# Building lists of token numbers on the chip instead of scattering them through DRAM, with w1 and w2 in two transfers each

## The chip, the cores and the metric

The kernel runs on one core of a Trainium2 chip. The engines are TensorE (PE; its weight loads are listed apart as PEld), VectorE (DVE), ScalarE (ACT), GpSimd (POOL) and SyncE (SP). PE's granted clock is 1.2 or 2.4 GHz; the profile gives it as a share of full speed, 0.50 or 1.00 or a mean of the two. The metric is the device time of one execution in microseconds; less is better.

## The reference, cut to what matters

```python
attn_out = _attn_ref(q, k, v)                 # 4 batches, 8 heads, 576 tokens, heads of 64
x = attn_out.transpose(0, 2, 1, 3).reshape(2304, 512)
# _moe_ref: 8 experts, capacity 576
expert_idx = np.argmax(x @ w_gate, axis=1)
for i in range(N):                            # in token order
    e = expert_idx[i]
    if counts[e] < capacity:
        disp[e, counts[e]] = x[i]; pos[i] = counts[e]; counts[e] += 1; keep[i] = True
h = np.maximum(np.einsum('ecd,edf->ecf', disp, w1), 0.0)    # w1 8 x 512 x 1024
y = np.einsum('ecf,efd->ecd', h, w2)                        # w2 8 x 1024 x 512
out[i] = gate_w[i] * y[expert_idx[i], pos[i]]               # kept tokens; others 0
# _moe2_ref
h = x @ w_in                                  # 512 x 2048
r = np.maximum(h, 0.0)
g = s * (r * r) + b
return g @ w_out                              # 2048 x 512
```

In `_attn_ref` keys and values are first averaged over 8 neighbours, so scores are 576 x 72. Of the 2304 tokens of these inputs 1663 are kept: 576, 0, 0, 571, 28, 0, 348 and 140 on the eight experts.

## The kernel before, in words

**Attention** goes through 4 batches of 5 tiles of tokens (128, the last 64). Of each tile it computes scores, values, gate logits, and writes the token's row of 512 values to `xd` in DRAM. For each batch (the last in two parts) `route` gives every token a slot: expert times `capp` plus its place in the expert, ranked by products with a triangular matrix on PE (L338, L340), finished on DVE (`rsf`, then `rsi`). Then POOL makes the token numbers (`iota`, L360) and writes them with an indirect DMA for each tile (L363, `ids<-tok,rsi`) to their slots in the DRAM list `ids`: 128 numbers of 4 bytes for each.

**Units.** The experts' tokens are worked off in units of 288 slots (CH). Units 0 and 1 are picked while attention still runs, after batches 1 and 2 (`pick`, `first.gather`); the other units come from a table that DVE computes once routing is complete (`make`, L595 to L716, ending with `u_ti`). Here there are five units (the last is "wide", 352 columns) and two small ones of up to 144. For each unit SP loads the 288 numbers (`idt`, 3 x 96; `idw` 64 more; `ids_s` for the small ones) from `ids`, and POOL gathers the rows of `xd` by them (`xg<-xd,idt`, L798). PE transposes the rows (`x_part`, L809), ACT and DVE split them into a high and a low part (`xs`, L810, L811), and each layer is three products (high by high, low by high, high by low): `layer1` L818, `layer2` L986. Weights are loaded by SP (`kraw` is w1, `vraw` is w2, each 2 MB in four transfers, L781 and L787) and split by ACT with POOL or DVE. Results go to `yt` in DRAM, and the unit's numbers to `idc` (L992: 288 numbers, from a tile with 96 partitions x 3, so each number is a piece of its own).

**Order.** The order on each engine is the order of the code. `layer1` of unit 0 stands beside the end of attention. `block(u)` is then `layer2` of unit u-1 with `x_part` of u, and `layer1` of u, f running over 8 chunks; beside it stand the splits and the conversion of the last layers' weights (`conv`; its loads `c_raw` are issued by ACT, L827, between ACT's own work). After the units come the small ones (L1099, L1106, L1114) and the last layers: seven blocks of 256 tokens through the second MLP (L912, L1282) with the rows read back from `yt`, scattered to the output by `idc`. `zeros` (L1029) clears the end of `yt` with four transfers.

**Counters.** The transfers that SP and ACT issue use eight counters, here called DMAHW0 to DMAHW7. A transfer that is to use a counter again first waits for the one that used it last, and its engine's queue stands meanwhile.

Of the kernel before, what the change touches and what calls it, by code (L numbers as in the profile page):

```python
# [45 lines left out]
def constants(nc, pool, capp):  # L46
# [24 lines left out]
    c.row0 = pool.tile([P, NB, E], F32, name="row0")  # L71
    nc.gpsimd.iota(c.row0, pattern=[[0, NB], [capp, E]], base=0, channel_multiplier=0, allow_small_or_imprecise_dtypes=True)
# [7 lines left out]
def attention(nc, tc, c, a, cap, capp, left, big, xd, ids, run, hist, first, ps0):  # L80
# [3 lines left out]
    with ExitStack() as es:  # L84
# [163 lines left out]
        def values(i, work=None):  # L248
# [9 lines left out]
            at_pe[0] = o[:, 1, 4 * VW:4 * VW + NB * E].rearrange("p (t e) -> p t e", e=E)  # L258
# [37 lines left out]
        def route(b, t0, t1):  # L296
# [40 lines left out]
            rk = at_pe[0][:, 0:w]  # L337
# [12 lines left out]
            nc.vector.tensor_add(sl, sl, c.row0[:, 0:w])  # L350
# [6 lines left out]
            si = tmp("rsi", [], I32)  # L357
            nc.vector.tensor_copy(si, sf)
            tok = tmp("tok", [], I32)
            nc.gpsimd.iota(tok, pattern=[[P, w]], base=b * S + t0 * P, channel_multiplier=1)  # L360
            for t in range(w):
                n = rows(t0 + t)
                i = nc.gpsimd.indirect_dma_start(out=ids, out_offset=bass.IndirectOffsetOnAxis(ap=si[:n, t:t + 1], axis=0),  # L363
                                                 in_=tok[:n, t:t + 1], in_offset=None, bounds_check=E * capp - 1, oob_is_err=False)
                tc.declare_no_dep(i.ins, group="scatter", reason="slots of different tokens")
                tc.add_to_no_dep_group("scatter", i.ins)
            if t1 == NB and b:

# [22 lines left out]

        o = ps1.tile([P, 2, 512], F32, name="o")
# [25 lines left out]
        for i, (b, t) in enumerate(tiles):  # L418
# [23 lines left out]
            if i == 1:  # L442
                first.fill(one)
# [39 lines left out]
        while todo or scales:  # L483
            more = 7
            while more and todo:
                more -= 1
                if step():
# [4 lines left out]
                    at_pe[0] = o[:, 1, 0:NB * E].rearrange("p (t e) -> p t e", e=E)  # L492
# [11 lines left out]
SSUB = SM // 2  # L504
# [14 lines left out]
class Table:  # L519
# [10 lines left out]
    def __init__(self, nc, pool, cap):  # L530
# [7 lines left out]
        self.st, self.g, self.io, self.iu, self.ie = t("st", [2, 2, E]), t("g", [J, E]), t("io", [J, E]), t("iu", [NV, E]), t("ie", [E, E])  # L538
# [5 lines left out]
        self.left, self.next, self.eq, self.num = t("left", [E]), t("next", [E]), t("eq", [E, E]), t("num", [4])  # L544
# [6 lines left out]
        iota(self.io, [[CH, J], [0, E]], SM)  # L551
        iota(self.iu, [[1, NV], [0, E]])
        iota(self.ie, [[0, E], [1, E]])
        iota(self.e1, [[1, E]], 1)

    def pick(self, nc, i, tot, rev, cap, capp):
# [28 lines left out]
        v.tensor_copy(self.i[i], f)  # L585

    def make(self, nc, hist, capp):
# [73 lines left out]
        units = lambda out, x: (v.tensor_tensor(out=out[:, :NV], in0=self.iu, in1=row(x[:, 0], NV), op=ALU.is_ge),  # L661
                                v.tensor_tensor(out=out[:, NV:], in0=self.ie.rearrange("p a b -> p b a"), in1=row(x[:, 1], E), op=ALU.is_ge))
# [5 lines left out]
        v.tensor_sub(mine, mine, cmp)  # L668
        ex, slot, col, new = (self.tab[:, i] for i in range(4))
# [23 lines left out]
        v.tensor_sub(ch, self.iu[:, :, 0], self.s2[:, 0:NV])  # L693
# [22 lines left out]
        v.tensor_copy(self.ti, self.tab)  # L716

# [31 lines left out]
class Experts:  # L749
# [4 lines left out]
    def __init__(self, nc, tc, c, a, left, m, xd, ids, idc, yt, hist, cap, capp):  # L754

        self.__dict__.update({k: v for k, v in locals().items() if k != "self"})
        self.t = Table(nc, left, cap)
# [11 lines left out]
        self.idt = [m.tile([SUB, NSUB], I32, name=f"idt{i}") for i in range(3)]  # L769
        self.w1v = a["moe_w1"].rearrange("e (k p) (f c) -> e p f k c", p=P, c=2 * P)  # L770
        self.w2v = a["moe_w2"].rearrange("e (f p) d -> e p f d", p=P)
        self.ids_s = [m.tile([SSUB, 2], I32, name=f"ids_s{i}") for i in range(4)]
# [6 lines left out]
    def load_w1(self, src):  # L779
        for i in range(KF // 2):  # L780
# [145 lines left out]
    def main(self, left, one, ps):  # L926
# [561 lines left out]
```

## Time and profile before

| | |
|---|---|
| three runs | 705.03, 713.31, 713.93 us, median 713.31 |
| the profiled execution | 706.86 us, span 705.1 us, mean granted clock 0.93 |
| busy: PE, DVE, ACT, POOL | 594.7, 382.1, 254.3, 324.2 us |
| attention | 0 to 122 us |
| unit 0, layer 1, beside the end of attention | 122 to 145 us |
| block 1, 2, 3, 4 | from 145, 185, 222, 268 to 302 us |
| small units and the last unit's layer 2 | 302 to 381 us |
| last layers: their start, then the rest | 381 to 424, 424 to 697 us |

A stage's PE busy time beside its length tells how much PE idles there; the row before a piece of idle time names what ended it. The profiled execution took 6.45 us less than the median of the three runs.

### The profile page before, as it was taken

Reading aid. Unit: us, or ns where it says so; the run is one execution under the profiler, and the core shown is the slowest. Engines: PE = TensorE matmul, PEld = TensorE weight load, DVE = VectorE, ACT = ScalarE, POOL = GpSimd, SP = SyncE. Lnnn points to the kernel's source line nnn. Section 1 sums busy time; section 2 is a strip of 40 time slices with the busy share of each in tenths; the row PEclk is TensorE's granted clock in tenths of the full one; section 3 lists DMA queues with packets and bytes.
Section 4 is the critical chain, followed back from the end, with each engine's and each line's share of the span. In section 5 each row is a group of like instructions: output and inputs, shape, how many; then the busy total and the mean of one; then the engine's idle time right before and its main releaser. Section 6 shows DMA issues by size and latency. Waiting matters only on the chain. (4 is left out here: it accounts for less than half of the span.)

```text
span 705.1 us, 11212 instructions
## 1 busy us (share of the span) xinstructions
PE 594.7 (84%) x3943; PEld 551.3 (78%) x3943; DVE 382.1 (54%) x793; ACT 254.3 (36%) x617; POOL 324.2 (46%) x336
## 2 busy tenths in 40 slices
PE   6887869769599387995879669989999999999985
PEld 5786768658499387995878648887989989899875
DVE  4686877949589382444422976998322113021150
ACT  1363645435254244424312634331413304123030
POOL 5566744565363343502310975544563515335291
PEclk8798998979889798999889879999999999999999
DMA  8998998692538776494824910001720100100000
GB/s 170 196 174 152 137 156 238 155 281 61 97 92 185 240 169 211 55 278 124 272 51 125 381 51 1 0 1 45 269 91 16 31 30 1 46 17 2 33 2 18
DMA packets 78572, 81.98 MB, mean 116 GB/s; under 512 B 30732, under 2 KB 59404, under 8 KB 78476
## 3 DMA queue, kind: packets, MB, share of 16 engines
q1 hardware_dynamic: 67580, 67.19, 37.7%
q0 software_dynamic: 3184, 6.83, 4.5%
q10 hardware_dynamic: 7712, 6.84, 3.3%
q8 instruction: 41, 0.67, 0.5%
q14 instruction: 55, 0.45, 0.4%
HBM read 64.04 MB, written 17.62 MB: 116 GB/s over the span
## 5 line engine op out<-in xcount | busy, mean ns | idle before, releaser
L1282 PE MATMUL bank<-wo,gh 128*128 128x512 f32 (+1 forms) x448 | 135.5, 385 | 15.3 <-POOL wo L1256 9.2
L1277 POOL TENSOR_TENSOR gl<-rt,gh 128x256 fp32r<-128x256 f32 (+1 forms) x112 | 89.4, 807 | 88.0 <-ACT gh L1276 80.7
L1282 PEld LDWEIGHTS bank<-wo,gh 128*128 128x128 f32 x448 | 83.6, 193 | 34.2 <-POOL wo L1256 11.1
L1282 PE MATMUL bank<-wo,gl 128*128 128x512 f32 (+1 forms) x224 | 85.7, 382 | 0.0
L791 POOL TENSOR_TENSOR w1l<-kraw,w1h 128x512 fp32r<-128x512 f32 x40 | 54.1, 1367 | 60.9 <-ACT w1h L790 60.6
L986 PE MATMUL bank<-hs,w2h 128*128 128x288 f32 (+1 forms) x308 | 73.4, 328 | 6.8 <-issue 6.8
L986 PEld LDWEIGHTS bank<-hs,w2h 128*128 128x128 f32 x308 | 55.4, 209 | 7.6 <-issue 7.3
L1289 DVE SCALAR_TENSOR_TENSOR raw<-bank,sb,c_u 128x512 f32<-128x512 f32 (+1 forms) x14 | 9.9, 710 | 85.4 <-PE bank L1282 85.4
L1270 ACT ACTIVATE rt<-tq 128x256 f32<-128x256 f32 (+1 forms) x26 | 9.6, 368 | 114.5 <-PE tq L912 92.7
L1282 PEld LDWEIGHTS bank<-wo,gl 128*128 128x128 f32 x224 | 43.3, 193 | 7.7
L986 PE MATMUL bank<-hs,w2l 128*128 128x288 f32 (+1 forms) x148 | 47.1, 318 | 0.0
L1276 ACT CAST gh<-rt 128x256 fp32r<-128x256 f32 (+1 forms) x112 | 43.0, 384 | 4.2 <-DVE rt L1271 4.1
L1271 DVE SCALAR_TENSOR_TENSOR rt<-bank,rt 128x256 f32<-128x256 f32 (+1 forms) x60 | 24.1, 402 | 36.1 <-ACT rt L1270 36.1
L1290 POOL DMA_INDIRECT out_dram<-raw,it x12 | 12.0, 1000 | 62.6 <-DVE raw L1289 62.1
L1270 ACT ACTIVATE rt<-bank 128x256 f32<-128x256 f32 (+1 forms) x60 | 22.2, 370 | 39.2 <-PE bank L912 26.2
L1256 POOL TENSOR_TENSOR wo<-c_f,wo 128x512 fp32r<-128x512 f32 x16 | 24.8, 1550 | 21.5 <-ACT wo L1255 21.5
L210 PE MATMUL sc<-kbd,qT 128*128 128x144 f32 (+1 forms) x152 | 26.3, 324 | 8.9 <-DVE r L267 6.2
L795 DVE TENSOR_TENSOR w2l<-vraw,w2h 128x512 fp32r<-128x512 f32 x39 | 32.3, 829 | 1.5 <-POOL tok L360 1.3
L798 POOL DMA_INDIRECT xg<-xd,idt x15 | 17.8, 1189 | 32.4 <-DMA idt<-ids 29.6
L986 PEld LDWEIGHTS bank<-hs,w2l 128*128 128x128 f32 x148 | 30.9, 209 | 0.0
L210 PEld LDWEIGHTS sc<-kbd,qT 128*128 128x128 f32 (+1 forms) x152 | 22.6, 206 | 10.5 <-issue 9.6
L255 PE MATMUL o<-vx,eT 128*128 128x146 f32 (+1 forms) x144 | 24.4, 317 | 6.6 <-DVE u_sum L569 3.1
(409 smaller groups left out, 1672.0 us busy)
## 6 DMA issues: line engine op xcount, KB each, us to landing
kraw<-in_moe_w_dram SPq DMA_DIRECT2D x24, 512.0 KB
vraw<-in_moe_w_dram SPq DMA_DIRECT2D x24, 512.0 KB
wo<-in_moe_w_out_dram SPq DMA_DIRECT2D x16, 512.0 KB
c_raw<-in_moe_w_in_dram ACTq DMA_DIRECT2D x13, 512.0 KB
kraw<-in_k_dram SPq DMA_DIRECT2D x8, 576.0 KB
out_dram<-c_u SPq DMA_DIRECT2D x1, 4608.0 KB
q<-in_q_dram SPq DMA_DIRECT2D x16, 256.0 KB
xd<-xr SPq DMA_DIRECT2D x16, 256.0 KB
```

Source lines behind the costliest of these rows:

```text
L210: nc.tensor.matmul(sc[:n, p // 2, p % 2 * 144:p % 2 * 144 + 144], lhsT=q[:, p, :n], rhs=kbd[b % 2][:, p], start=True, stop=True)
L255: nc.tensor.matmul(o[:n, p // 2, p % 2 * 2 * VW:p % 2 * 2 * VW + 2 * VW], lhsT=et[:, p, :n], rhs=two_cols(vx[g][:, 2 * p:2 * p + 2]), star ...
L791: eng.tensor_sub(self.w1l[:, i], self.w1(i), self.w1h[:, i])
L795: eng.tensor_sub(self.w2l[i], self.w2r[:, i], self.w2h[i])
L798: self.nc.gpsimd.indirect_dma_start(out=self.xg[u % 2][:, s], out_offset=None, in_=self.xd[:rows], in_offset=bass.IndirectOffsetOnAxis(ap= ...
L986: nc.tensor.matmul(py[d][:, :v.n], lhsT=l[f][:, d * P:d * P + P], rhs=r[f], start=f == 0 and i == 0, stop=f == KF - 1 and i == 2)
L1256: nc.gpsimd.tensor_sub(w[:, 1], f, w[:, 0])
L1270: nc.scalar.activation(r, p, AF.Relu)
L1271: nc.vector.scalar_tensor_tensor(out=r, in0=p, scalar=0.0, in1=r, op0=ALU.max, op1=ALU.mult)
L1276: nc.scalar.copy(gh[:, at, :n], rt[f % 4][:, :n])
L1277: nc.gpsimd.tensor_sub(gl[:, at, :n], rt[f % 4][:, :n], gh[:, at, :n])
L1282: nc.tensor.matmul(p[:, c], lhsT=l[:, at, j * P:j * P + P], rhs=wo[f][:, z, c], start=f == 0 and i == 0, stop=f == KF2 - 1 and i == 2)
```

## The change

Four things change. **The lists.** `ids` in DRAM goes, with its scatters and the loads `idt`, `idw`, `ids_s`. For each batch POOL now divides the slot into a multiple of 96 and a remainder (six small operations on `rsf`) and makes two one-hot matrices for each tile, `ohq` (128 x 48: which row of 96) and `ohp` (128 x 96: which place in it, times the token's number). PE adds `ohq` transposed times `ohp` over the tiles (L394), and DVE adds that to `u_lists`, 48 rows of 96 numbers in SBUF. A unit's numbers are a selection of rows by a further product: `picked` (L631) for units 0 and 1, `numbers` (L642) for all others at once, after the table; DVE turns them into indices in SBUF that the gathers use directly. **The store to `idc`** comes from a tile with rows of 96 numbers (L879): three pieces of 384 bytes for a unit, not 288 of 4 bytes. **w1 and w2** come in two transfers of 1 MB each, not four of 512 KB; rows of w1 are 2 KB, not 1 KB. **`zeros`** is one transfer, not four, and `idc` is filled at the start. `capp` falls from 864 to 576. The units of these inputs stay the same.

```diff
@@ route
-            si = tmp("rsi", [], I32)
-            nc.vector.tensor_copy(si, sf)
-            tok = tmp("tok", [], I32)
-            nc.gpsimd.iota(tok, pattern=[[P, w]], base=b * S + t0 * P, channel_multiplier=1)
+            g = nc.gpsimd
...
+            g.tensor_scalar(out=qi, in0=sf, scalar1=1.0 / SUB, scalar2=None, op0=ALU.mult)
+            g.tensor_scalar(out=key, in0=qi, scalar1=float(-SUB), scalar2=None, op0=ALU.mult)
+            g.tensor_add(lo, key, sf)
+            g.tensor_scalar(out=key, in0=lo, scalar1=0.0, scalar2=float(SUB), op0=ALU.is_lt, op1=ALU.mult)
+            g.tensor_add(lo, lo, key)
+            g.tensor_sub(key, sf, lo)
+            g.iota(tok, pattern=[[P, w]], base=b * S + t0 * P, channel_multiplier=1, allow_small_or_imprecise_dtypes=True)
             for t in range(w):
-                n = rows(t0 + t)
-                i = nc.gpsimd.indirect_dma_start(out=ids, out_offset=bass.IndirectOffsetOnAxis(ap=si[:n, t:t + 1], axis=0),
-                                                 in_=tok[:n, t:t + 1], in_offset=None, bounds_check=E * capp - 1, oob_is_err=False)
...
+                g.tensor_scalar(out=ohq[:, t], in0=q96, scalar1=key[:, t:t + 1], scalar2=None, op0=ALU.is_equal)
+                g.tensor_scalar(out=ohp[:, t], in0=p96, scalar1=lo[:, t:t + 1], scalar2=tok[:, t:t + 1], op0=ALU.is_equal, op1=ALU.mult)
...
+            n = at_pe[0][:nq, NB * E:NB * E + SUB]
+            for t in range(w):
+                m = rows(t0 + t)
+                nc.tensor.matmul(n, lhsT=ohq[:m, t], rhs=ohp[:m, t], start=t == 0, stop=t == w - 1)
+            lists = first.t.lists
+            if b:
+                nc.vector.tensor_add(lists, lists, n)
+            else:
+                nc.vector.tensor_copy(lists, n)
+            if last and b < B - 1:
...
+                first.t.picked(nc, b - 1, at_pe[0][:SUB, NB * E + SUB:NB * E + SUB + 4])
+                while scales:
+                    scale()
+                first.gather(b - 1, b * S + S)
@@ Table
+    def picked(self, nc, i, p):
+        nc.tensor.matmul(p, lhsT=self.lists, rhs=self.sel[:self.lists.shape[0]], start=True, stop=True)
+        nc.vector.tensor_add(self.pf[:SUB, i], p, self.over[:SUB])
+        nc.vector.tensor_copy(self.idx01[:SUB, i], self.pf[:SUB, i])
...
+    def numbers(self, nc, c, p, rows):
...
+        nc.tensor.matmul(p[:SUB, 0:w], lhsT=self.lists, rhs=sel[:n], start=True, stop=True)
+        nc.vector.scalar_tensor_tensor(out=idx[:SUB], in0=over[:SUB], scalar=float(BIG), in1=p[:SUB, 0:w], op0=ALU.mult, op1=ALU.add)
+        yield
+        nc.vector.tensor_copy(self.idx[:SUB].rearrange("p u s -> p (u s)"), idx[:SUB])
+        yield
+        nc.tensor.transpose(p[:w, P:P + SUB], idx[:SUB], c.ident[:SUB, :SUB])
+        nc.scalar.copy(rows[:w], p[:w, P:P + SUB])
@@ make, at its end
         v.tensor_copy(self.ti, self.tab)
+        four = lambda x: x.unsqueeze(2).to_broadcast([P, NV + E, 4])
+        sel, over, s4 = (self.flat(z).rearrange("p (u s) -> p u s", s=4) for z in (mine, cmp, p2))
+        v.tensor_tensor(out=s4, in0=four(slot), in1=self.at.unsqueeze(1).to_broadcast([P, NV + E, 4]), op=ALU.add)
+        yield
+        v.tensor_tensor(out=over, in0=s4, in1=four(self.lim), op=ALU.subtract)
+        v.tensor_scalar(out=sel, in0=s4, scalar1=self.p96, scalar2=None, op0=ALU.is_equal)
+        yield
+        v.tensor_scalar(out=over, in0=over, scalar1=self.atp[:, 0:1], scalar2=0.0, op0=ALU.add, op1=ALU.is_ge)
@@ Experts
     def load_w1(self, src):
-        for i in range(KF // 2):
+        for i in range(KF // 4):
             self.nc.sync.dma_start(out=self.w1r[:, i], in_=src[:, i])
     def load_w2(self, src, i):
-        self.nc.sync.dma_start(out=self.w2r[:, i:i + 2], in_=src[:, i:i + 2])
+        self.nc.sync.dma_start(out=self.w2r[:, i:i + 4], in_=src[:, i:i + 4])
...
-    def load_ids(self, u, slots):
-        self.nc.sync.dma_start(out=self.idt[u % 3], in_=slots.rearrange("(s p) o -> p (s o)", p=SUB))
+    def gather(self, u, have):
+        for s in range(NSUB):
+            self.rows(self.xg[u % 2][:, s], self.t.idx01[:, u, s:s + 1], have)
+    def store_numbers(self, u, i, n, rows):
+        self.nc.sync.dma_start(out=self.idc[bass.ds(self.regs[u][1], n * SUB)].rearrange("(s p) o -> s (p o)", p=SUB), in_=rows[4 * i:4 * i + n])
...
-            nc.sync.dma_start(out=self.idc[cols(u, ids.shape[1] * sub)].rearrange("(s p) o -> p (s o)", p=sub), in_=ids)
...
-            for k in range(KD):
-                nc.sync.dma_start(out=yt[k * P:k * P + P, bass.ds(self.kept, 2 * CU)].rearrange("p (n c) -> p n c", c=CU),
-                                  in_=zf.unsqueeze(1).to_broadcast([P, 2, CU]))
+            nc.sync.dma_start(out=yt.rearrange("(d p) n -> p d n", p=P)[:, :, bass.ds(self.kept, 2 * CU)], in_=zf.unsqueeze(1).to_broadcast([P, KD, DM]))
@@ block
+                    lists = self.t.numbers(nc, self.c, px[0], rows)
+                if u == 1 and f > 4:
+                    next(lists, None)
+                if u == 1 and f == 7:
+                    tokens(2, 0)
...
-                if u == 1 and 0 <= f - 3 <= NSUB:
-                    tokens(2, f - 3)
+                if u == 1 and f < NSUB:
+                    tokens(2, f + 1)
```

On POOL, batch 0 before: the two operations of its list stand between the pooling of keys and of values.

```order
L138 TENSOR_TENSOR kraw<-kraw 72x4x128
L140 TENSOR_TENSOR kp<-kraw 72x256
L360 IOTA tok_842 128x5
L363 DMA ids<-tok_842,rsi_840 7008x1 x5
L136 TENSOR_TENSOR vraw<-vraw 128x4x256
L138 TENSOR_TENSOR vraw<-vraw 128x4x128
```

The same place now; the pair L374, L375 stands five times.

```order
L147 TENSOR_TENSOR kp<-kraw 72x256
L366 TENSOR_SCALAR rqi_851<-rsf_838 128x5
L367 TENSOR_SCALAR rkey_853<-rqi_851 128x5
L368 TENSOR_TENSOR rlo_852<-rkey_853,rsf_838 128x5
L369 TENSOR_SCALAR rkey_853<-rlo_852 128x5
L370 TENSOR_TENSOR rlo_852<-rlo_852,rkey_853 128x5
L371 TENSOR_TENSOR rkey_853<-rsf_838,rlo_852 128x5
L372 IOTA tok_854 128x5
L374 TENSOR_SCALAR ohq<-q_198,rkey_853 128x48
L375 TENSOR_SCALAR ohp<-p_199,rlo_852,tok_854 128x96
L374 TENSOR_SCALAR ohq<-q_198,rkey_853 128x48
L375 TENSOR_SCALAR ohp<-p_199,rlo_852,tok_854 128x96
```

Seventeen instructions stand where there were six, and PE has a product (L394) behind them. On PE the end of layer 1 of unit 0 now holds the last ranks and list of batch 3 in this order, ahead of block 1's first product (L1047).

```order
L894 MATMUL misc<-xs,w1l 128x288
L345 LDWEIGHTS tri
L345 MATMUL o<-roh_1844,tri 128x16
L347 LDWEIGHTS ones
L347 MATMUL o<-roh_1844,ones 128x8
L348 LDWEIGHTS ones
L348 MATMUL o<-run,ones 128x16
L383 LDWEIGHTS ones
L383 MATMUL o<-run,ones 128x8
L394 MATMUL o<-ohp,ohq 48x96 x2
L1282 MATMUL tq<-ident,u_pf 8x96
L1047 MATMUL bank_1901<-hs,w2h_162 128x288 x2
```

Before, the ranks of the first part of batch 3 (L338) stood after the first of the eight chunks of that layer, and those of the second part after the fourth; now the first stand after the fifth and the second at the very end, and a list (L394) follows each. On ACT, block 3 before (waits in brackets; DMAHW are the transfers' counters): between two pieces of `xs` stands a load of `c_raw` that waits for a counter.

```order
L810 CAST xs<-tq 128x288 [waits DVE_49,PE_49]
L790 CAST w1h<-kraw 128x512 [waits DMAHW3_49,Pool_49]
L737 ACTIVATE c_u_1894<-c_raw_1114 128x512 [waits DMAHW0_49]
L827 DMA c_raw_1029<-in_moe_w_in_dram 128x4x256 [waits DMAHW2_49,Activation_49]
L810 CAST xs<-misc 128x288 [waits DVE_49,PE_49]
L790 CAST w1h<-kraw 128x512 [waits Pool_49]
```

On SP just ahead of block 3 now: one transfer of zeros (L1084), then w2 (L859) in two; the loads of `idt` and `idw` that stood ahead of the zeros are gone.

```order
L1084 DMA yt<-raw_1917 128x4x512 [waits DMAHW6_49,DMAHW2_49,DVE_49]
L1257 COMPARE_AND_BRANCH
L1036 TENSOR_LOAD u_ti
L1036 ISA x2
L1095 COMPARE_AND_BRANCH
L859 ISA
L859 DMA vraw<-in_moe_w_dram 128x4x512 [waits DMAHW0_49,DMAHW7_49,DVE_49,Activation_49]
```

ACT's load there still waits for DMAHW2, but w2 uses counters 0 and 1, and DMAHW2 belongs to the store of unit 1's results, half a block earlier.

## Rows read from the trace of the kernel before

**Rows 1.** Windows: length; PE, PEld, DVE, ACT, POOL busy; PE clock, DMA share, GB/s
```profile
76.00:122.00 46.00, 39.46 (x298) 36.05 (x296) 36.17 (x121) 26.52 (x55) 23.72 (x22) 0.93 1.05 178
...
222.00:268.00 46.00, 28.88 (x206) 28.20 (x204) 28.06 (x36) 16.11 (x35) 16.25 (x12) 0.85 0.80 228
268.00:302.00 34.00, 33.43 (x216) 32.60 (x217) 13.72 (x24) 17.10 (x37) 14.67 (x12) 0.95 0.52 110
...
424.00:697.00 273.00, 264.56 (x1722) 240.14 (x1720) 108.96 (x184) 78.23 (x229) 124.83 (x146) 1.00 0.11 38
```

**Rows 2.** Timeline of PE: start, length, work, idle time before it and its releaser
```profile
74.86 1.24 PE L255 MATMUL o<-vx,eT 128*128 128x146 f32 x8 [2.41 <-DVE rsf L355]
...
98.92 1.24 PE L255 MATMUL o<-vx,eT 128*128 128x146 f32 x8 [3.08 <-DVE u_sum L569]
...
151.90 0.42 PE L809 MATMUL tq<-ident,xg 96*128 96x96 f32 x1 [3.21 <-DMA xg<-xd,idt]
...
176.62 0.53 PE L818 MATMUL bank<-xs,w1h 128*128 128x288 f32 x2 [2.07 <-DVE hs L821]
...
190.29 0.39 PE L809 MATMUL tq<-ident,xg 96*128 96x96 f32 x1 [4.90 <-DMA xg<-xd,idt]
...
240.25 0.74 PE L809 MATMUL misc<-ident,xg 96*128 96x96 f32 x3 [11.05 <-DVE xs L811]
...
267.95 0.82 PE L986 MATMUL bank<-hs,w2h 128*128 128x288 f32 x2 [5.93 <-issue]
...
335.05 1.22 PE L1114 MATMUL bank<-rt,vraw 128*128 128x144 f32 x8 [3.48 <-issue]
...
361.16 5.14 PE L1114 MATMUL bank<-rt,vraw 128*128 128x144 f32 x20 [3.67 <-issue]
```

**Rows 3.** Waits of PE: releaser, us in total, times, longest
```profile
PE tq L809 <- DMA xg<-xd,idt: 12.8, 5, 4.9
...
PE bank L1106 <- DVE yr L1100: 3.9, 2, 2.8
```

**Rows 4.** Timeline of DVE: the first and the last of the table's work in block 1
```profile
165.17 1.38 DVE L647 TENSOR_TENSOR u_tri<-u_key 128x128 f32<-128x128 f32 x1
...
176.00 0.20 DVE L716 CAST u_ti<-u_tab 128x76 int32<-128x76 f32 x1
```

**Rows 5.** Timeline of ACT in block 3
```profile
239.31 0.40 ACT L810 CAST xs<-misc 128x288 fp32r<-128x288 f32 x1 [13.93 <-DMA vraw<-in_moe_w_dram]
```

**Rows 6.** Timeline of SP's transfers from block 2 to block 3: start, length of the issues
```profile
210.34 0.43 SPq L992 DMA_DIRECT2D idc<-idt  x1
...
223.57 0.34 SPq L803 DMA_DIRECT2D idt<-ids  x1
...
229.02 3.67 SPq L1029 DMA_DIRECT2D yt<-rt  x4
234.03 2.32 SPq L787 DMA_DIRECT2D vraw<-in_moe_w_dram  x4
```

**Rows 7.** Windows before, in and after the time that follows a store of `idc`
```profile
205.00:212.00 7.00, 7.00 (x55) 7.00 (x54) 6.83 (x7) 4.04 (x9) 6.47 (x6) 1.00 0.60 183
213.00:221.00 8.00, 8.00 (x63) 8.00 (x62) 8.00 (x12) 4.70 (x10) 3.19 (x3) 1.00 0.70 53
222.00:228.00 6.00, 6.00 (x51) 6.00 (x50) 5.41 (x9) 2.45 (x6) 1.28 (x1) 1.00 1.08 352
...
288.00:303.00 15.00, 15.00 (x95) 15.00 (x94) 9.91 (x17) 8.33 (x17) 3.43 (x3) 1.00 0.58 44
```

**Rows 8.** Groups of instructions by line on POOL: busy us, mean ns, idle before
```profile
L363 POOL DMA_INDIRECT ids<-tok,rsi x20 | 20.1, 1003 | 13.4 <-issue 6.3 <-DVE xr L293 6.0 <-POOL tok L360 0.8
...
L70 POOL TENSOR_SCALAR pen<-pen 128x40 f32<-128x40 f32 x1 | 0.3, 324 | 0.0
```

**Rows 9.** The chain that ended last, its first two pieces: start, us
```profile
373.21 7.28 DMA idc<-ids_s
380.63 4.35 DMA wo<-in_moe_w_out_dram
```

More of the change, by code (lines that the diff above doesn't have):

```diff
@@ L77, in rows, with attention @@
     return P if t < NB - 1 else S - (NB - 1) * P
-def attention(nc, tc, c, a, cap, capp, left, big, xd, ids, run, hist, first, ps0):
+def attention(nc, tc, c, a, cap, capp, left, big, xd, run, hist, first, ps0):
     with ExitStack() as es:
@@ L390, in attention @@
         pool_all("k", 0, 7, 8, nc.gpsimd)
+        first.nc.sync.dma_start(out=first.idc.rearrange("(p n) o -> p (n o)", p=SUB), in_=big_ids)
         o = ps1.tile([P, 2, 512], F32, name="o")
@@ L679, in make @@
         v.memset(new, 0.0)
+        v.tensor_tensor(out=p2[:, 0:NV + E], in0=mine, in1=row(self.ends, NV + E), op=ALU.mult)
         v.tensor_reduce(out=ex, in_=ohe, axis=AX.X, op=ALU.add)
@@ L683, in make @@
         yield
+        v.tensor_reduce(out=self.lim, in_=p2[:, 0:NV + E], axis=AX.X, op=ALU.add)
         v.tensor_tensor(out=new[:, 1:], in0=ex[:, 1:], in1=ex[:, :NV + E - 1], op=ALU.not_equal)
@@ L827, in load_raw @@
             queue.dma_start(out=self.c_raw[i % 3].rearrange("p (k c) two -> p k (c two)", k=KD), in_=self.w_in64[:, (KF + i) % KF2])
-    def fill(self, pool):
-        nc = self.nc
-        for d, w in ((self.ids, E * self.capp // SUB + 1), (self.idc, (T + 2 * CH) // SUB)):
-            z = pool.tile([SUB, w], I32, name=f"z{w}")
-            nc.gpsimd.iota(z, pattern=[[1, w]], base=BIG, channel_multiplier=0)
-            nc.sync.dma_start(out=d.rearrange("(p n) o -> p (n o)", p=SUB), in_=z)
     def beside(self, i, pool):
@@ L891, in unit1 @@
         self.picked(1)
-        for s in range(NSUB):
-            self.gather(1, s, T - S)
     def load_y(self, u):
@@ L940, in main @@
         wide = self.Parts(WIDE, mem[:2 * KD], mem[2 * KD:])
-        idw = [left.tile([MORE, 1], I32, name=f"idw{i}") for i in range(3)]
         self.it = [left.tile([P, 2], I32, name=f"it{i}") for i in range(4)]
@@ L947, in main @@
         yo = lambda i, n: ys[:, i * KD * CH:i * KD * CH + KD * n].rearrange("p (k c) -> p k c", k=KD)
-        zf = self.rt[0]
+        zf = self.raw[0]
+        rows, rows01 = (self.yr[:, i, SM:SM + SUB].bitcast(I32) for i in range(2))
         xs = self.yr[:, :, 0:SM]
@@ L1041, in block @@
                 with if_new(u - 2):
-                    for f in range(0, KF, 2):
+                    for f in range(0, KF, 4):
                         self.load_w2(w2s(u), f)
@@ L1128, in to_small @@
             small_gather(0)
-            if v is wide:
-                nc.sync.dma_start(out=self.idc[CH:][cols(u, MORE)], in_=idw[u % 3])
             with if_new(self.t.NV):
@@ L1168, in last @@
             early = cap >= SM + CU
+            small_numbers(s)
             if early:
@@ L1449, in program @@
         xd = dr.tile([T, DM], F32, name="xd")
-        ids = dr.tile([E * capp + SUB, 1], I32, name="ids")
         idc = dr.tile([T + 2 * CH, 1], I32, name="idc")
@@ L1458, in program @@
             with tc.tile_pool(name="m", bufs=1, side="right") as m:
[L1459 to L1460 removed]
+                x = Experts(nc, tc, c, a, left, m, xd, idc, yt, hist, cap, capp)
+                ps = attention(nc, tc, c, a, cap, capp, left, m, xd, run, hist, x, ps0)
                 w = es.enter_context(tc.tile_pool(name="w", bufs=1))
```

169 lines of the change are left out of this document (95 added, 74 removed).

## The prediction

> **What bounds the kernel now.** I read the windows by stage first. From 424 us on, PE is busy 264.56 of 273 us at full clock [rows 1]: nothing in this change touches that, so whatever comes must come from the 424 us ahead of it. In block 3 (222 to 268 us) PE is busy only 28.88 of 46 us, at a granted clock of 0.85, and block 4 next to it is full (33.43 of 34) [rows 1]. So the second view was PE's timeline there. Two holes make up 17 us: 11.05 us ahead of an `x_part` product, and 5.93 us at the block's end [rows 2]. The first is put down to DVE's `xs`, which waits for ACT's `xs`, which sat 13.93 us until a load of w2 (`vraw`) had landed [rows 5]. ACT's `xs` needs no w2. What needs it is the load of `c_raw` that stands ahead of it on ACT: it waits for the counter DMAHW2, last used by w2, as the order of ACT shows. And w2 was late because SP issued it only at 234.03 us, behind four transfers of zeros that went out from 229.02 to 232.69, behind `idt` at 223.57 and `idw` [rows 6]. The second hole ends on "issue", with another such `c_raw` load ahead of the work that PE waits for.
>
> The third view was the rate of the transfers. After SP stores `idc` at 210.34 us [rows 6], the rate falls from 183 to 53 GB/s for 8 us though the DMA engines are 0.70 busy, then rises to 352; after the wide unit's store it is 44 GB/s for 15 us at a share of 0.58 [rows 7]. Busy engines that move little are moving small pieces: the 288 numbers are 288 pieces of 4 bytes. The scatters of `ids` are 128 such pieces each. I call this the crawl. The last store of that kind heads the chain that ended last: 7.28 us, and only then does the load of `wo` (4.35 us) start that the last layers wait for [rows 9].
>
> **The change part by part**, against the profiled execution, 706.86 us.
>
> *Block 3's holes.* The changed order has one transfer of zeros, no `idt` or `idw` ahead of w2, and ACT's load of `c_raw` waits for the counter of a store that went out half a block earlier. I take both holes as gone, 11.05 + 5.93, and of the low clock beside them 1.5 us: −18.5. Next in line there is the split of w1 on ACT and POOL; block 4, which does the same work, has no such hole [rows 1]. A load of w1 or w2, now 1 MB in a piece, lands later at its first half: 512 KB more at 183 to 352 GB/s [rows 7] are 1.5 to 2.9 us. If that falls at the head of both halves of a block, and the clock with it, half the gain is left: −9 is the smaller bound.
>
> *Waits for gathers.* PE waited 12.8 us in five pieces for gathers of units 1 and 2 [rows 3], whose lists were scattered, read back, then used. Now indices stand in SBUF and this goes, −12.8 before what replaces it.
>
> *What replaces it.* POOL's price for a small operation is 0.32 us (a tensor_scalar of 128 x 40), that of a scatter 1.0 us [rows 8]. A list of five tiles is 17 operations of 0.3 us and 0.07 us between dependent ones, 6.3 us; before it was 5 scatters and their gaps, 6.4 us. POOL's time is neutral, but before nobody waited for it, and now PE stands in order at L394.
> - Batch 0: `rsf` comes at 74.86 us [rows 2], the list at about 81, and PE arrives one tile later, at 76.6: +4.5.
> - Products L394 (20 tiles), L631, L642, and DVE's adds: 0.25 us a tile by the three 96 x 96 transposes of 0.74 us [rows 2], half of it beside other waits: +2.
> - End of layer 1 of unit 0: ranks, total and list of batch 3 now stand at the end of the row, and PE waits for DVE's slots and POOL's one-hots of the second part, some 4 us for the first list (three tiles, 4.8 us of POOL) and 6 for the second. +10.
> - Table: its bulk on DVE runs from 165.17 to 176.20 [rows 4], and PE waited 2.07 us for DVE behind it [rows 2]. Now eight more operations of 0.2 to 0.3 us stand there, and PE stands at L642 after the sixth chunk until they are done, 10.5 us where it could go on before; the 2.07 go. +8.5.
>
> Sum from 145 to the start of block 3: 10 + 8.5 − 12.8 = +6 (rounded), with bounds of −5 (DVE finds its inputs earlier and PE waits little) and +15 (each list takes twice as long).
>
> *The crawl gone.* The stores are now three pieces of 384 bytes, the scatters none. In attention the 3.08 us at 98.92 [rows 2] stood behind a store of `xr` in the crawl of batch 1's scatters: −3. After the stores of the small units, PE waits 3.48 and 3.67 us for "issue" [rows 2], time in which instructions come late; I take −5 of these and a third, smaller one. PE waited 3.9 us for `yr` at the small unit's start [rows 3], again behind ACT and a w2 load: −4. At the last layers' start `wo` no longer waits out the 7.28 us [rows 9]; a contiguous store still takes 2 to 3: −4.5. Half-clock time after the holes that go, beyond what block 3 has: −4. Together −20.5.
>
> One rule speaks against this. The Trainium skill, "DMA: Bandwidth & Descriptors", section Specifications, gives 512 B as the least transfer for line rate and says that below this the engine does a read-modify-write. The new pieces, 384 bytes, are still below it; by that rule alone the crawl would stay, and the sum would be 20.5 us worse but for the yr wait. The rows show only 4-byte pieces, and there are 96 times fewer now, so I take their number as what costs and leave the other reading to a rival.
>
> *w1 and w2 in half as many transfers.* Same bytes; a 2 KB row moves little faster than two of 1 KB, and SP's queue is not what fills the time. The gain is the counters, counted above. Nothing else.
>
> Sum: −18.5 + 4.5 + 2 + 6 − 20.5 = −26.5, so 680 us on the profiled execution's basis. The median of the three runs stands 6.45 us above it and two of the three lie there, so I add 6: **686 us**.
>
> **The rivals.** 2% of 713.31 (about what a measurement here can tell from no change) puts the borders at 699.0 and 727.6.
>
> *The crawl stays.* Small pieces, those of 384 bytes included, hold the queues as before whatever their number, and only the counters' waits go. For it: the rows cannot tell number from size. Against it: 3 pieces instead of 288. (It is what the rule of the Trainium skill above would make of these stores.) Then the −20.5 shrinks to −4 (the `yr` wait is one of counters): −10, 697 on the profile's basis, 703 on the median's: within 2%.
>
> *The units end earlier but the last layers do not start earlier.* Conversion of their weights on DVE, ACT and POOL stands between the units' work and may fill the time instead; in block 3 DVE is busy 28.06 of 46 us [rows 1], so without the holes it is nearly as full as PE. If half of block 3's gain and half of the crawl's is lost that way: 686 + 9 + 10 = 705; if only block 3's, 695. I take 697.
>
> *Slower: PE waits for POOL's one-hots.* Four lists stand on PE's path (batch 0, batch 2 beside layer 1, two of batch 3). If a small POOL operation costs 1.0 us, as an indirect transfer does [rows 8], a list of five takes 17 us, not 6.3, and one of three 13. That is +10.7 for batch 0 and for batch 2 (whose cover is one chunk of 2 us, gone then), +8 and +6 for the others, 35 us, and as much as 5 more of table start: −26.5 + 40 = +13.5, 727 on the median's basis, the border of slower. It decides from about 0.75 us an operation, where the sum is zero. For it: POOL spans stretch beside a busy DVE. Against it: 0.32 us measured.
>
> **How the numbers follow.** Forecast .66, of which nearly all lies under 699 (its own range 668 to 699); last layers not earlier .14 (697, half under 699, half over); the crawl stays .13 (703, a third under 699); slower .07 (727, and .05 of it beyond 727.6). Faster: .63 + .08 + .04 = .75; same .20; slower .05. The lower end is every listed hole gone with new waits at their lower bounds: 686 − 11 − 9 − 4 = 662; the upper one takes in the crawl's rival, 706.
>
> **What would show it.** Right: no PE hole over 3 us from 222 to 302 us of the old order; no window of 8 us under 60 GB/s at a DMA share over 0.5 behind a store of `idc`; a PE wait of 4 to 5 us for POOL at L394 in batch 0, of 8 to 12 us for DVE at L642; no wait for gathers of units 1 and 2. Wrong would make me: `c_raw` loads on ACT that still wait for w2; POOL operations beyond 0.6 us; the crawl behind three pieces of 384 bytes; or a larger gain in attention, where DMA share is 1.05 from 76 to 122 us [rows 1], if the transfers, not PE's chain, set its length.

## The result, and the profile after

The changed kernel took 679.5 us (median of 4 runs, 678.86 to 680.74), the kernel before in the same runs 711.82: a ratio of 0.9564, 95% interval 0.9495 to 0.9632. The profiled spans are 677.1 and 705.1 us, 28.0 less. The forecast was 686, from −26.5 on the profiled execution. Where the sets of runs below hold slow runs of the kernel before (over 1.5% above its fastest), the medians count them and the ratios leave them out.

First the page of the changed kernel: PE's line, PE's clock in 40 slices, and the packets.

```profile
PE 598.0 (88%) x3991; PEld 550.0 (81%) x3991; DVE 386.9 (57%) x814; ACT 254.6 (38%) x619; POOL 330.0 (49%) x391
...
PEclk8798699886789998999999779999999999999999
...
DMA packets 65887, 81.92 MB, mean 121 GB/s; under 512 B 24698, under 2 KB 40058, under 8 KB 65793
```

PE's work has not shrunk, 598.0 us against 594.7; its share rose because the span fell. Where the time went is read from the starts of the stages in the two timelines of PE:

| stage starts at (first product of) | before, us | after, us | stage that ends here: after less before, us |
|---|---|---|---|
| layer 1 of unit 0 (L818, now L894) | 129.16 | 129.19 | 0.0 |
| block 1 (L986, now L1047) | 144.47 | 159.34 | +14.8 |
| block 3 | 221.84 | 230.79 | −5.9 |
| block 4 | 267.95 | 260.97 | −15.9 |
| small units (L1106, now L1163) | 317.49 | 310.70 | +0.2 |
| last layers (L912, now L974) | 371.92 | 348.73 | −16.4 |
| their second layer (L1282, now L1344) | 402.61 | 373.85 | −5.6 |
| end of span | 705.1 | 677.1 | +0.8 |

So the stage in which the lists are finished became twice as long, and the change pays in block 3, the small units and the start of the last layers. The rows of PE's timeline in the changed kernel that answer to [rows 2] (idle time and its releaser in brackets):

```profile
76.09 0.55 PE L394 MATMUL o<-ohp,ohq 128*48 128x96 f32 x2 [1.06 <-POOL ohp L375]
...
145.71 0.37 PE L394 MATMUL o<-ohp,ohq 128*48 128x96 f32 x2 [2.57 <-POOL ohp L375]
...
157.30 0.55 PE L394 MATMUL o<-ohp,ohq 128*48 128x96 f32 x2 [3.66 <-POOL ohp L375]
...
185.18 0.60 PE L642 MATMUL tq<-u_mine,u_lists 48*96 48x76 f32 x2 [13.26 <-DVE u_mine L788]
...
260.97 0.51 PE L1047 MATMUL bank<-hs,w2h 128*128 128x288 f32 x2 [2.98 <-issue]
...
320.62 1.22 PE L1171 MATMUL bank<-rt,vraw 128*128 128x144 f32 x8 [1.92 <-issue]
...
340.91 4.16 PE L1171 MATMUL bank<-rt,vraw 128*128 128x144 f32 x32 [1.60 <-issue]
```

No hole of 11 us is left in block 3, and the 5.93 at its end are 2.98; the waits for "issue" among the small units have halved ("issue" means that the profile shows nothing that the engine waited for). In their place stand waits for POOL's one-hots and one of 13.26 us for the table. What the waits for the lists do to the clock is in the windows of the same kernel, columns as in [rows 1]:

```profile
140.00:145.00 5.00, 3.14 (x24) 2.91 (x22) 3.35 (x13) 2.15 (x5) 3.97 (x11) 1.00 0.68 221
145.00:150.00 5.00, 3.11 (x13) 2.35 (x14) 1.01 (x6) 0.83 (x2) 2.75 (x5) 0.60 0.00 2
150.00:155.00 5.00, 1.96 (x11) 1.58 (x9) 2.29 (x14) 1.13 (x2) 0.65 (x3) 0.50 0.14 52
155.00:160.00 5.00, 2.02 (x8) 1.25 (x9) 0.25 (x1) 0.69 (x3) 3.56 (x10) 0.50 0.78 254
```

From 143 us PE works and waits by turns, and the granted clock falls from 1.00 to 0.50: the chunk of layer 1 in the middle of it runs at half speed as well.

SP's transfers and the windows behind the store of `idc` answer to [rows 6, 7]:

```profile
219.19 0.34 SPq L879 DMA_DIRECT2D idc<-yr  x1
221.24 4.13 SPq L853 DMA_DIRECT2D kraw<-in_moe_w_dram  x2
227.00 0.41 SPq L1084 DMA_DIRECT2D yt<-raw  x1
228.53 6.05 SPq L859 DMA_DIRECT2D vraw<-in_moe_w_dram  x2
```

```profile
218.00:226.00 8.00, 7.93 (x61) 7.70 (x59) 7.86 (x8) 4.42 (x12) 6.55 (x6) 1.00 0.82 268
226.00:234.00 8.00, 8.00 (x62) 8.00 (x63) 8.00 (x17) 5.32 (x12) 0.17 (x1) 1.00 1.04 315
234.00:245.00 11.00, 10.92 (x86) 10.69 (x85) 10.90 (x15) 7.06 (x16) 9.42 (x7) 1.00 1.02 349
```

Where 53 GB/s followed the store before, 268 and 315 follow it now. The first transfer of w2 goes out 1.5 us after the zeros.

The chain that ended last no longer has a store of `idc` at the last layers' start:

```profile
349.33 3.21 DMA yt<-yo
...
352.80 4.06 DMA wo<-in_moe_w_out_dram
```

It waits 3.21 us for the last results' store, where it waited 7.28 [rows 9].

### The profile page after: what moved, and what is told of

Read it like the earlier page. It is cut to its first block, busy times and chain, and to the rows that moved or that the text cites. A ratio compares the mean times of both kernels' runs of the same rounds, so it can differ in the third digit from the quotient of the medians.

```text
span 677.1 us, 11128 instructions
## 1 busy us (share of the span) xinstructions
PE 598.0 (88%) x3991; PEld 550.0 (81%) x3991; DVE 386.9 (57%) x814; ACT 254.6 (38%) x619; POOL 330.0 (49%) x391
## 4 chain that ended last, share of the span: by engine, by line
PE 42%; DVE 20%; issue 6%; POOL 3%; DMA 3%; ACT 2%; SPq 0%; DVEq 0%; another core or an unknown queue 0%; ACTq 0%; POOLq 0%
PE bank L1344 13%; PE bank L974 7%; PE bank L1047 6%; DVE c_f L1367 4%; PE tq L974 4%; PE misc L974 4%; PE bank L894 3%; DVE c_f L814 2%; DVE w2l L867 2%; DVE c_f L812 1%; DVE c_f L809 1%; PE misc L894 1%; PE tq L894 1%; DVE c_f L818 1%; POOL gl L1339 1%
## 5 line engine op out<-in xcount | busy, mean ns | idle before, releaser
L1344 PE MATMUL bank<-wo,gh 128*128 128x512 f32 (+1 forms) x448 | 136.3, 387 | 11.7 <-POOL wo L1318 8.5
L1344 PEld LDWEIGHTS bank<-wo,gh 128*128 128x128 f32 x448 | 83.9, 194 | 30.8 <-POOL wo L1318 10.5
L1344 PE MATMUL bank<-wo,gl 128*128 128x512 f32 (+1 forms) x224 | 86.2, 385 | 0.0
L863 POOL TENSOR_TENSOR w1l<-kraw,w1h 128x512 fp32r<-128x512 f32 x40 | 52.6, 1331 | 47.3 <-ACT w1h L862 46.9
L1047 PE MATMUL bank<-hs,w2h 128*128 128x288 f32 (+1 forms) x308 | 71.3, 321 | 3.2 <-issue 3.0
L1047 PEld LDWEIGHTS bank<-hs,w2h 128*128 128x128 f32 x308 | 53.3, 202 | 4.2 <-issue 3.6
L1344 PEld LDWEIGHTS bank<-wo,gl 128*128 128x128 f32 x224 | 43.6, 195 | 7.9
L1047 PE MATMUL bank<-hs,w2l 128*128 128x288 f32 (+1 forms) x148 | 46.2, 312 | 0.0
L871 POOL DMA_INDIRECT xg<-xd,u_idx x24 | 26.3, 1094 | 24.3 <-DVE u_idx L645 10.9
L867 DVE TENSOR_TENSOR w2l<-vraw,w2h 128x512 fp32r<-128x512 f32 x39 | 30.4, 779 | 1.4 <-ACT w2h L866 1.0
L1047 PEld LDWEIGHTS bank<-hs,w2l 128*128 128x128 f32 x148 | 29.8, 201 | 0.0
L1367 DVE TENSOR_TENSOR c_f<-c_f,wo 128x512 f32<-128x512 f32 x30 | 26.3, 877 | 0.8
```

What stands on the lines that cost most here:

```text
L863: eng.tensor_sub(self.w1l[:, i], self.w1(i), self.w1h[:, i])
L867: eng.tensor_sub(self.w2l[i], self.w2r[:, i], self.w2h[i])
L871: self.nc.gpsimd.indirect_dma_start(out=dst, out_offset=None, in_=self.xd[:have], in_offset=bass.IndirectOffsetOnAxis(ap=idx[:n], axis=0), ...
L1047: nc.tensor.matmul(py[d][:, :v.n], lhsT=l[f][:, d * P:d * P + P], rhs=r[f], start=f == 0 and i == 0, stop=f == KF - 1 and i == 2)
L1344: nc.tensor.matmul(p[:, c], lhsT=l[:, at, j * P:j * P + P], rhs=wo[f][:, z, c], start=f == 0 and i == 0, stop=f == KF2 - 1 and i == 2)
L1367: nc.vector.tensor_add(sums["acc"], sums["acc"], wo[i // 2][:, i % 2])
```

## The experiments

All times are medians; "before" is the kernel before on the same chip in the same runs; a set is what ran on one chip together. The kernel before moved from set to set (711.8, 714.3, 724.0, 719.7, 724.5), so kernels are compared within a set, or by their ratio.

**The small pieces put back.** In the changed kernel the numbers go to `idc` from the tile of 96 partitions x 3 again.

```diff
-        self.nc.sync.dma_start(out=self.idc[bass.ds(self.regs[u][1], n * SUB)].rearrange("(s p) o -> s (p o)", p=SUB), in_=rows[4 * i:4 * i + n])
+        idx = self.t.idx01[:, u] if isinstance(u, int) and u < 2 else self.t.idx[:, i]
+        self.nc.sync.dma_start(out=self.idc[bass.ds(self.regs[u][1], n * SUB)].rearrange("(s p) o -> p (s o)", p=SUB), in_=idx[:SUB, 0:n])
```

> The changed kernel, with one thing undone: the numbers go to idc from the tile with 96 partitions x 3, 288 pieces of 4 bytes, not three of 384. If small pieces make the crawl, windows behind each store fall under 80 GB/s again, the waits for issue among the small units and the late start of the last layers come back, and it takes 8 to 16 us more than the changed kernel, 688 to 695. If the counters of the transfers made the gain, it stays at 679 to 682.

696.43 us (before 714.34; 0.9773, 0.9698 to 0.9847), a little above the 688 to 695 expected. Windows of this kernel behind two of the stores (the first, longer one takes in transfers from before the rate falls), and then PE's holes:

```profile
220.00:228.00 8.00, 7.97 (x60) 7.74 (x60) 7.86 (x12) 4.94 (x12) 4.80 (x4) 1.00 0.95 110
223.00:230.00 7.00, 6.97 (x53) 6.74 (x52) 7.00 (x13) 4.61 (x11) 1.99 (x2) 1.00 0.67 37
...
290.00:297.00 7.00, 7.00 (x45) 7.00 (x44) 4.46 (x8) 3.71 (x8) 1.33 (x2) 1.00 0.97 56
```

```profile
268.78 0.82 PE L1048 MATMUL bank<-hs,w2h 128*128 128x288 f32 x2 [7.78 <-issue]
...
353.55 5.83 PE L1172 MATMUL bank<-rt,vraw 128*128 128x144 f32 x32 [4.03 <-issue]
```

The rate is 110 GB/s at a share of 0.95 from 220 to 228 us and 37 at 0.67 from 223 to 230; the hole at the end of block 3 is 7.78 us, the wait for "issue" among the small units 4.03. Seven stores are worth about 17 us beside the changed kernel's 679.5 of another set, and still 12 beside the kernel with four transfers (below), which ran in the same set and took 683.99.

**Rows of `idc` alone,** in the kernel before, copied from `ids` inside DRAM. The wide unit's further 64 numbers are copied the same way.

```diff
-            nc.sync.dma_start(out=self.idc[cols(u, ids.shape[1] * sub)].rearrange("(s p) o -> p (s o)", p=sub), in_=ids)
+            n = ids.shape[1] * sub
+            nc.sync.dma_start(out=self.idc[cols(u, n)].rearrange("(s p) o -> s (p o)", p=96 if n == CH else 72), in_=self.ids[bass.ds(regs[u][1], n)].rearrange("(s p) o -> s (p o)", p=96 if n == CH else 72))
```

> The kernel before, with one thing done: idc is copied from ids inside DRAM in rows of 96 or 72 numbers, not written from SBUF in pieces of 4 bytes. If small pieces make the crawl, 8 to 14 us less than before, 698 to 704, while the holes of 11 and 6 us in block 3 stay; if only the counters matter, no difference, 708 to 714.

684.46 us, 0.958 (0.9505 to 0.9656), where 698 to 704 was expected: these few lines bring nearly as much as the whole change. And the holes of block 3, which I expected to stay, went, though zeros, w2 and the loads of `idt` stand in the old order. PE's timeline of this kernel, and its windows behind the load of `idt` at 224.71 us:

```profile
236.73 0.56 PE L809 MATMUL misc<-ident,xg 96*128 96x96 f32 x3 [2.87 <-DVE xs L811]
...
260.57 0.57 PE L986 MATMUL bank<-hs,w2h 128*128 128x288 f32 x2 [2.06 <-issue]
```

```profile
224.00:231.00 7.00, 6.97 (x55) 6.74 (x54) 7.00 (x15) 3.34 (x7) 1.45 (x1) 1.00 0.92 282
231.00:240.00 9.00, 6.13 (x38) 5.90 (x37) 5.69 (x7) 3.64 (x8) 3.88 (x4) 0.83 0.91 298
```

11.05 became 2.87, 5.93 became 2.06. The counters' queue is still there; it costs little when nothing in it is slow. In the kernel before, the zeros stood on SP until a transfer of w1 had landed, as SP's waits from 195 to 250 us show:

```profile
SPq L1029 <- DMA kraw<-in_moe_w_dram: 4.8, 2, 3.2
```

That w1 went out from 212.29 us, right behind the store of `idc` at 210.34, in the stretch of 53 GB/s [rows 7].

**Four transfers each, in the changed kernel** (w1, w2 and the zeros).

```diff
-            self.nc.sync.dma_start(out=self.w1r[:, i], in_=src[:, i])
+            for j in range(0, 4 * P, 2 * P):
+                self.nc.sync.dma_start(out=self.w1r[:, i, :, j:j + 2 * P], in_=src[:, i, :, j:j + 2 * P])
...
+        for j in (i, i + 2):
+            self.nc.sync.dma_start(out=self.w2r[:, j:j + 2], in_=src[:, j:j + 2])
...
+            for k in range(KD):
+                nc.sync.dma_start(out=yt[k * P:k * P + P, bass.ds(self.kept, 2 * CU)], in_=zf)
```

> The changed kernel with w1, w2 and the zeros in four transfers each again. If the counters' waits made the holes of block 3, ACT waits there again for a load of w2 and it takes 10 to 17 us more, 690 to 697. If the holes came from the crawl behind the stores, or from the loads of idt and idw ahead of w2, it stays at 679 to 682.

683.99 us (0.9585, 0.9504 to 0.9666), some 4 more than the changed kernel in other sets, where 10 to 17 more was expected. ACT does wait for w2 again, as the timeline shows, but short:

```profile
237.46 0.40 ACT L888 CAST xs<-misc 128x288 fp32r<-128x288 f32 x1 [3.10 <-DMA vraw<-in_moe_w_dram]
```

3.10 us, not 13.93 [rows 5].

**Two transfers and one of zeros, in the kernel before;** scatters, lists and stores of `idc` as they were. The edit is that of the change in `load_w1`, `load_w2`, their callers and `zeros`.

```diff
-        for i in range(KF // 2):
+        for i in range(KF // 4):
...
-        self.nc.sync.dma_start(out=self.w2r[:, i:i + 2], in_=src[:, i:i + 2])
+        self.nc.sync.dma_start(out=self.w2r[:, i:i + 4], in_=src[:, i:i + 4])
```

> The kernel before with w1 and w2 in two transfers and the zeros in one; lists, scatters and stores of idc as before. If the counters' waits made the holes of block 3, they go and it takes 12 to 18 us less than before, 694 to 700; if the crawl made them, they stay and it takes 709 to 714.

694.45 us, 0.9754 (0.9668 to 0.984). The hole of 11 us is gone, since no `c_raw` load waits for w2; the one at the end of block 3 is not:

```profile
263.24 0.82 PE L986 MATMUL bank<-hs,w2h 128*128 128x288 f32 x2 [7.30 <-issue]
```

So either cure takes the first hole: it needed a slow transfer and a queue behind it. The second hole goes by the stores alone. Two transfers leave it (7.30), rows of `idc` take it (2.06), and it is back where 4-byte pieces are put back (7.78 above). What PE waits for in it the profile does not name, so the way from the store to PE stays open there.

**Both cures without the lists.**

> The kernel before with both parts done that need no new lists: idc in rows, copied inside DRAM, and w1 and w2 in two transfers, the zeros in one. Scatters of ids and the loads idt, idw, ids_s stay. If the lists on the chip are worth nothing in the sum (waits for gathers gone, waits for lists come), 676 to 682, as the changed kernel: the 30 us of the one part and the 20 of the other share the 17 us of block 3's holes. If the lists bring the rest, 684 to 690, no better than the rows of idc alone.

678.31 us; its set's before was 724.0, the ratio 0.9395 (0.9316 to 0.9474). The changed kernel, in a set with 724.52, had 0.9397 (below). The lists on the chip are worth nothing in the sum, within a percent. They move time about. PE's timeline of this kernel without them, and waits of ACT (100 to 135 us) and SP (90 to 140 us):

```profile
128.16 0.69 PE L243 MATMUL te<-ident,s 64*128 64x64 f32 x4 [10.50 <-ACT eT L246]
...
163.90 0.39 PE L809 MATMUL tq<-ident,xg 96*128 96x96 f32 x1 [5.38 <-DMA xg<-xd,idt]
```

```profile
ACT w1h L790 <- DMA kraw<-in_moe_w_dram: 11.6, 1, 11.6
...
SPq L803 <- DMA ids<-tok,rsi: 9.9, 1, 9.9
```

A wait of 10.50 us at the end of attention and 5.38 for a gather; layer 1 of unit 0 starts at 136.33 us (129.19 with the lists) but block 3 at 228.06 (230.79). The wait of 10.50 starts at the scatters: SP stands 9.9 us at the load of `idt` until they have landed, the loads of unit 0's w1 stand behind it, and ACT waits 11.6 us for them ahead of `eT`. The two kernels before with one cure show the same (SP waits 6.6 and 6.4 us, PE 6.41 and 4.46); in the kept trace of the kernel before, one of its shorter executions, SP waits 0.5. So the lists do remove a wait at the end of attention, which the stage table above cannot show; what they add later takes it back.

**Which pieces are slow.** Behind each store of `idc` the changed kernel makes one more, of 288 pieces of 4, 64 or 512 bytes (w = 1, 16 or 128 numbers), to a spare list that nobody reads.

```diff
+        self.nc.sync.dma_start(out=self.junk.rearrange("(s p) c -> p s c", p=SUB), in_=self.c.ident[:SUB, 0:w].unsqueeze(1).to_broadcast([SUB, 3, w]))
```

> The changed kernel with one more store for each unit right behind the store to idc: 288 pieces of 4 bytes into a spare list in DRAM that nobody reads. If small pieces themselves make the crawl, 690 to 698 as with the 4-byte store to idc; if only a store that others wait for costs, 680 to 683.

> The same with 288 pieces of 64 bytes. If every piece below the size for line rate costs alike (the Trainium skill, DMA: Bandwidth & Descriptors, Specifications, sets it at 512 B), 690 to 698; if it is 4-byte pieces alone, 680 to 684.

> The same with 288 pieces of 512 bytes, as control for the extra transfer and its counter: 680 to 684 by every theory in which size matters; 690 or more if the number of pieces of a store is what costs, whatever their size.

4 bytes: 701.21 us, above the 690 to 698 expected. 64 bytes: 680.26. 512 bytes: 680.95. All three on one chip. Windows of the first behind two of its stores:

```profile
222.00:229.00 7.00, 6.93 (x52) 6.70 (x51) 6.90 (x10) 4.26 (x9) 4.25 (x4) 1.00 0.73 93
229.00:231.00 2.00, 2.00 (x18) 2.00 (x17) 2.00 (x5) 0.99 (x3) 0.00 (x0) 1.00 0.55 20
...
290.00:306.00 16.00, 16.00 (x101) 16.00 (x101) 10.64 (x19) 8.45 (x17) 1.97 (x2) 1.00 0.49 98
```

and of the second, at the same places of the program:

```profile
222.00:229.00 7.00, 6.93 (x52) 6.70 (x51) 6.90 (x9) 4.33 (x10) 4.38 (x4) 1.00 0.93 269
229.00:231.00 2.00, 2.00 (x18) 2.00 (x17) 2.00 (x6) 0.97 (x3) 0.00 (x0) 1.00 1.04 400
...
283.00:299.00 16.00, 16.00 (x101) 16.00 (x100) 10.63 (x19) 8.64 (x18) 2.37 (x3) 1.00 0.82 262
```

The same number of pieces, 16 times the bytes, and 269 GB/s in place of 93. What costs is the piece of 4 bytes, 21 us for seven stores, and not their number. The hole at the end of block 3 is back too:

```profile
268.96 0.82 PE L1048 MATMUL bank<-hs,w2h 128*128 128x288 f32 x2 [7.72 <-issue]
```

The spare list holds its pieces one behind the other, so 16 pieces of 4 bytes share the stretch of DRAM that one of 64 fills. Whether the size of a piece costs or such neighbours do, no run tells.

**The waits for the lists.** In the first kernel L642 and what follows stand behind the fourth chunk of layer 1 of unit 1; in the second the last batch's lists are made on DVE besides.

```diff
-                if u == 1 and f > 4:
-                    next(lists, None)
-                if u == 1 and f == 7:
-                    tokens(2, 0)
...
+                if u == 1 and f in (4, 5):
+                    next(lists, None)
+                if u == 1 and f == 5:
+                    next(lists, None)
+                    tokens(2, 0)
...
-            g = nc.gpsimd
+            g = nc.vector if b == B - 1 else nc.gpsimd
```

> The changed kernel with the numbers of the later units (the product L642 and what follows) behind the fourth chunk of layer 1 of unit 1, not behind the sixth of layer 2 of unit 0, and the gathers of unit 2 after it. If PE's wait of 13.3 us there is real cost, PE works on meanwhile and 6 to 9 us go: 671 to 674. If it only moves, because the gathers of unit 2 then come late for block 2, 678 to 681.

> The same, and the lists of the last batch are made on DVE, not on POOL (the running number stays on POOL). PE waits 2.6 to 4.9 us for each of the two lists at the end of layer 1 of unit 0 while DVE idles 4.3 us; with small operations of 0.17 to 0.25 us on DVE against 0.2 to 0.7 on POOL, 4 to 6 us less than with late numbers alone: 666 to 669. If the ranks on DVE ahead of the lists set that stage, no difference.

677.23 and 676.49 us on one chip (before 719.67; ratios 0.9414, 0.9376 to 0.9452, and 0.9408, 0.9364 to 0.9452): between them nothing that can be told, so the 4 to 6 us expected of the lists on DVE did not show. The first lies between its two theories (671 to 674, 678 to 681). In it the wait of 13.26 us became others:

```profile
179.18 0.61 PE L1047 MATMUL bank<-hs,w2l 128*128 128x288 f32 x1 [4.10 <-DVE w2l L867]
...
202.13 0.64 PE L885 MATMUL tq<-ident,xg 96*128 96x96 f32 x2 [3.33 <-DMA xg<-xd,u_idx]
```

PE now waits 4.10 us for a split that stands behind the table on DVE, and then for the gather of unit 2, which the table holds up as before; block 3 starts at 228.66 us, 2.1 earlier. So much of that wait only moved.

The changed kernel had not run on that chip, so both were run once more, side by side.

> The changed kernel as it is, on the chip of the next one, for a comparison side by side: 677 to 682.

> Late numbers and the last batch's lists on DVE, once more, beside the changed kernel on the same chip. If the 2 to 3 us between them were those two moves, it takes 2 to 4 us less than its neighbour again; if they were the chip, the two agree within 1.5 us.

680.63 us (679.27 to 682.43; 0.9397, 0.9349 to 0.9446) and 675.7 (674.25 to 680.4; 0.9346, 0.9293 to 0.9399): 4.9 less between the medians, a little above the 2 to 4 expected, though the intervals overlap, so that the two moves gain anything is likely and not shown. The lists' waits on DVE, from the timeline of the second:

```profile
145.91 1.06 PE L394 MATMUL o<-ohp,ohq 128*48 128x96 f32 x6 [2.02 <-DVE ohp L375]
...
154.90 1.04 PE L394 MATMUL o<-ohp,ohq 128*48 128x96 f32 x4 [2.89 <-DVE hist L385]
```

One wait of 2.02 for three tiles, where three waits of 2.57, 0.69 and 0.50 stood, and 2.89 for 3.66 and 0.50. This kernel has the lowest median of all that were tried beside the changed one.

## Why the prediction was right, and where its steps were not

*The total* came within 7 us of the forecast, and the profiled gain, 28.0, within 2 of the sum of −26.5. The 6.5 us between 686 and 679.5 are the 6 that were added for the median: the changed kernel's four runs lie within 2 us, so that its median stands beside its profiled execution.

Much of the agreement is luck, errors that cancel. The parts that are lists (4.5 + 2 + 6, and −3 for the scatters' crawl) came to +9.5, those of the two cures to −36. The kernel with both cures and no lists has a span of 677.2 us, 27.9 less than before, and the changed kernel 677.1. So on these single executions the cures were put some 8 us too high and the lists some 10 too dear.

*Block 3, −18.5.* Measured −15.9; the first hole went whole, the second to 2.98 us. The mechanism was told as the counters' alone, with −9 as the smaller bound if loads land later. The runs show two causes in a row for the first hole: the crawl delayed w1 (a wait of the zeros), the zeros delayed w2, and the counter passed that to ACT and PE. Rows of `idc` alone take that hole to 2.87 us, two transfers alone take it away. The second hole was put down to another `c_raw` load; it is the stores' alone, as two transfers leave it at 7.30 us. The order of waits was read rightly; that it starts at a store of 4-byte pieces 30 us earlier was not, though [rows 6, 7] show both within one stretch.

*The crawl, −20.5.* Right in kind: putting the pieces back costs 17 us beside the changed kernel of another set and 12 beside the kernel with four transfers of the same set; adding them costs 21. The sum's parts were off. The small units gave 16.4 us where I had −5 for issue and −4 for `yr` and part of the −4 for the clock; the last layers' start gave 5.6 for −4.5. In attention nothing came of −3, +4.5 and part of +2: the list of batch 0 held PE from 75.0 to 80.3 us as forecast (a wait of 1.06 and four of 0.5 us, with the products between; 3.0 us of waiting, below the 4 to 5 named as a sign), and the attention stage still ended at the same time as in the kept trace of the kernel before. That "issue" is time in which instructions come late was a reading of the word; no run shows it.

*The lists, +6 net from 145 us to block 3.* Measured +14.8 at the end of layer 1 and −5.9 from there, +8.9. The end of layer 1 was put at +10: the waits for POOL and DVE were about that (2.57, 0.69, 0.50, 1.07, 0.61, 3.66 and 0.50 make 9.6), but the products of the lists and the clock at 0.50 from 150 us came on top. Table and gathers were put at 8.5 − 12.8 = −4.3, the wait at L642 at 10.5 (a sign: 8 to 12); it was 13.26, and the waits for the gathers of units 1 and 2 did go. The two blocks together gave −5.9.

*POOL's price.* 0.32 us was taken for every small operation; the six on 5 numbers took 0.20 to 0.27, `ohq` 0.41 and `ohp` 0.70 with two scalars, so a list of five tiles took 7.1 us (73.05 to 80.2), not 6.3, or 0.42 an operation. The rival on this needed 0.75.

*w1 and w2 in two transfers, nothing but the counters.* Nearly right for the changed kernel: four again cost 4.5 us against the 679.5 of another set. In the kernel before, two were worth 20 us, because there a slow queue stood behind the counters: with rows of `idc` in place they took 684.46 to 678.31, 6 us between two sets.

*The rivals.* That the crawl stays with pieces of 384 bytes did not happen; neither did the last layers refuse to start earlier. The rule of the Trainium skill that spoke for the first (DMA: Bandwidth & Descriptors, Specifications: below 512 B a read-modify-write, no line rate) does not tell these sizes apart: the runs show no loss at 64 bytes and 21 us at 4.

## What to carry to other kernels

A store in which each piece is a single 4-byte number was cheap where it was issued (0.35 to 0.44 us on SP with the pieces put back) and dear for everything behind it: read the rate of the transfers (GB/s beside the DMA share) in the 10 us after each small store, and if it falls, make the pieces rows. When an engine waits for a load that it does not use, look at the queue and at the counter of the transfer ahead of it, and then at what made that transfer late; curing any one link may take the whole wait, so that a hole with two cures is gained once. (The two cures here brought 4.2% and 2.5% alone and 6.1% together, short of the sum by less than the intervals can tell; their other gains lie apart.) A list that is moved from DRAM to the chip brings waits of its own: the waits for scatters and gathers go, but asynchronous scatters become products in PE's order, and here the sum was nothing.

## What the runs showed of the hardware that was not expected

- In the windows shown behind two of the extra stores, 288 pieces of 4 bytes leave all transfers together 20 to 98 GB/s over 9 and 16 us, at a DMA share of 0.49 to 0.73; with 288 pieces of 64 bytes it is 262 to 400 at the same places. The cost by size has a step between 4 and 64 bytes; where, no run here shows.
- A read of the same list in pieces of 4 bytes had no such wake: in the kernel before with rows of `idc` alone, which still loads `idt` at 224.71 us, the transfers made 282 GB/s from 224 to 231 us and 298 from 231 to 240. Nor had its copy inside DRAM in rows at 214.48 us: 279 GB/s from 215 to 223.
- The kernel before moved between 705.0 and 729.2 us over sets and chips, the changed one only between 678.9 and 682.4.
